# A hand-searched order for the first 930 operations, replaced by another

## The chip, the cores and the metric

The kernel runs on one core of a Trainium2 chip. The metric is the device time of one launch in microseconds (us), the median of three runs. The engines are TensorE (PE; PEld is its weight load), VectorE (DVE), ScalarE (ACT), GpSimd (POOL) and SyncE (SP), which issues all loads and stores here.

## What is computed

A linear attention with a decaying state, and two gated layers behind it, all in float32 accuracy:

```python
for t in range(S):                                    # B, H, S, D = 4, 8, 768, 48
    cur = einsum('bhd,bhe->bhde', u * k[t], v[t])
    y[t] = einsum('bhd,bhde->bhe', r[t], state + cur)
    state = w[t][..., None] * state + einsum('bhd,bhe->bhde', k[t], v[t])
x  = y, transposed to (3072 tokens, 384)
x1 = ((x @ w_a) * (x @ w_b)) @ w_out                  # d_ff 1536
out = (max(x1 @ w_in, 0) ** 2) @ w_out2               # d_ff 2048
```

## The kernel before

**Attention** is done for 24 pairs of chunks of 64 time steps. For each pair the kernel loads `ef` (the decays, L281), `rk` (r and k transposed, L285), `nat` (r and k as they are, L289) and v in two layouts (`vs`, L292 and 293; `v`, L298). DVE forms the running products of the decays (a scan, L307) and their reciprocals (four L312); k and r are scaled by them (L316 and L326, on DVE or GpSimd), and the diagonal terms come from two products on `nat` (L337), a sum (L341) and two L350. PE makes the scores (L361, L362), a transpose of k (L372), the state's increment (L384, L386) and the result (L405, L406); DVE merges scores and diagonal (L367) and updates the state (L393 to L397); ACT copies the result out of PSUM (`ys`, L230), and SP stores it to DRAM (L417).

**The layers** take the tokens in blocks: 384, 256, 384 and four of 512 in the first, six of 512 in the second. A block's x is loaded from DRAM (L692), and held as two rounded float32 parts whose sum is x: ACT makes the high part `xh` (L230), and an L631 subtracts it to leave `xl`. Each product is then three matmuls instead of one (L431 to L433). In a block of the first layer there are twelve steps f. A step makes two products ("ua" and "ub"); ACT evacuates the first (L438), DVE multiplies it with the second (L442), ACT and DVE or GpSimd split the result into `gh` (L230) and `gl` (L454), and nine matmuls add it to three accumulators (L461 to L463, the "down" matmuls). The accumulators are evacuated at the block's end (L230 or L234) and stored (L688).

**The weights** are float64 words. A unit of weights serves a step; three loads bring it (L219), and seven operations decode it: two copies on ACT, a mask (L248), a shift (L252), an addition (L257), a copy on ACT, and a subtraction (L266) that leaves the low part. L257 and L266 go to DVE or GpSimd. All of the first layer's twelve units are decoded during block 0.

**The order.** The program first lists 2574 operations (`plan.add`), each with the engines that can do it, and a list scheduler (`Plan.run`) puts them in an order with times of its own. The first 930 in that order are then replaced by a table, `LEAD`: numbers of operations, in the order in which they are written into the program, with a letter for the engine (V DVE, A ACT, P POOL; without one it is PE or a DMA, of which there is one choice). The engines run what is written for them strictly in this order, SP too, and each instruction waits for its operands and for its buffer. The 930 reach to the second step of block 3, some 270 us into the run.

```python
lead = [(int(x.rstrip("VAP")), LETTER.get(x[-1])) for x in LEAD.split()]
led = {i for i, _ in lead}
order = [(0.0, i, e or next(iter(ops[i][1]))) for i, e in lead] + [x for x in order if x[1] not in led]
```

Of the kernel before, what the change touches and what calls it, by code (L numbers as in the profile page):

```python
# [49 lines left out]

LETTER = {"V": "DVE", "A": "ACT", "P": "POOL"}
LEAD = """
    0 4 34 5V 2573 31 6V 8V 7V 35 1 16P 36V 62 2572 17V 47P 9V 11P 2 37V 32 10P 696 48P 14A 12A 39V 38V 18V 24 40V 66
# [4 lines left out]
    926A 91 730A 90A 746 106V 927V 722V 108P 118A 105A 928 133V 131V 142V 723P 729A 92 114 737 116V 96 724A 929A 137V
    731V 931 125 747 119V 139P 930P 932A 732V 115 738 933V 733V 756 934 120A 725V 748 734A 135V 936 126 757 122 766
    935A 132V 130V 735P 943 739A 937V 138A 121A 938A 945 741V 740A 134V 939V 749A 148 742V 758 776 149A 751V 940 767  # L60
    750A 944A 743V 941 946V 744A 752V 159 942 145 144 952 745V 953A 947A 759A 954 753P 760A 150V 777 768 961 955V
    761V 963 786 948V 962A 754A 762V 949 770A 970 971A 778 136A 950 755V 763P 787 127 158 806 796 964V 769A 147V 972
    956A 979 951 965A 973V 771V 764A 957V 772V 780A 958 788 981 797 123 980A 765V 146 966V 773V 779A 974A 774A 798
    982V 988 781V 975V 990 151A 775V 782V 959 967 989A 789A 152A 960 983A 790A 991V 155 976 968 969 977 157 807 791V
    783V 784A 997 984V 808 792V 153 985 998A 978 999 785V 171V 793V 799A 992A 1000V 794A 801V 986 1006 800A 154 993V
    1007A 1008 795V 112A 1048 189 802V 994 1001A 1009V 987 1015 803V 1002V 809A 1016A 1010A 186 1017 172V 995 804A
    1011P 1018V 1003 173V 996 811V 1004 1012 805V 1005 1013 810A 812V 1024 1019A 143A 813V 217 188 156 190 1026 1020V
    160V 1021 1014 814A 1025A 1049A 187 221 815V 1022 1023 1027V 1050P 1033 164V 163V 161V 1028A 1029P 1035 1034A
    191V 1030 1036V 1051 170P 1037A 195V 162V 1031 1052A 1053 1038P 166V 167A 1032 1060 165V 1054V 193V 202P 1039
    1061A 1042A 192V 1062 203P 179 1069 168V 180A 232P 1063V 176 1055A 1071 1070A 1064A 169A 175 204V 194V 1056P 222V  # L70
    181V 1072V 251 196P 1078 178V 174A 1079A 218 219 1065P 197P 1057 1040 210 225V 1041 177 1080 1073A 224V 200A 233P
    198A 211A 220 247 1044V 234V 226V 1043 201P 1066 1058 207 1081V 223V 199P 1074P 1046A 182A 212V 183A 1067 1087
    1088A 206 1059 1082V 262P 228P 205A 227P 209V 1089 1083P 1075 1096 240 1068 1090V 229V 184 279 275 249 1091A 241A
    1097A 263V 208 1098 1076 252V 213A 215 248 1045 1092V 1084 1105 280V 231P 230P 290P 255V 1099V 264V 307 185 237
    242V 1107 1106A 1077 236 1108V 260V 1114 1085 235A 239V 276 1116 1093 1100A 318P 1101P 258P 1115A 214A 1086 216
    238 253V 281V 254V 1117V 303 277 250 1094 291P 1123 256V 243A 259P 292V 245 1102 1124A 1109A 1125 335 257V 1095
    283V 1126V 1110P 1132 308V 319V 1103 268 1133A 244A 1118A 269A 1111 1104 1119V 288P 1112 1127A 282V 284V 1134 246
    1165 261P 1135V 312V 309V 278 1128P 1113 266 267V 1141 1136A 285P 1120 305 1142A 1143 346P 1144V 286P 296 270V
    1121 297A 1150 347P 1166A 1122 1152 310V 1151A 1167P 1153V 1145V 265A 294 289P 304 311V 320V 331 1129 298V 271A
    1168 1137P 287P 293A 1130 272A 1138 363 313V 1146V 336V 1169A 1170 1147 1139 1131 340V 1171V 316P 295V 374P 1148  # L80
    1140 1177 359 273 348V 324 337V 314P 332 333 1178A 1154A 391 325A 315P 1179 322 361 306 1047 1155P 1180V 339V
    338V 317P 364V 1186 402V 323V 1149 1187A 342P 1188 341V 1156 375P 1195 1189V 1172A 1181A 1159A 299A 300A 1173P
    344P 301 274 1157 1197 403P 345P 343P 1196A 326V 368V 376V 419 1158 352 1204 365V 1161V 1190V 353A 321A 387 360
    367V 334 366V 350 1174 1182P 1198V 302 1205A 430V 1191P 1206 327A 351V 329 1160 431P 1163A 1175 389 1213 1207V
    392V 370V 1176 1183 1199A 1215 369V 1214A 328A 354V 395V 1216V 380 1192 394V 372V 1222 404V 396V 349A 373V 388
    330 381A 1200V 393V 1162 1164 415 1184 378 355A 371V 382V 390 357 1223A 1224 1185 1208A 377A 356A 1193 1231 447
    362 417 443 1209V 1225V 399V 358 416 1201 397V 1233 1232A 398V 1194 408 1202 1240 409A 1217A 379V 400V 432V 1218V
    1203 1210 475 1282 406 1211 1226A 420V 458V 1227V 383A 459V 1234V 401V 445 418 1219 410V 1212 384A 1228 1220 1242
    1221 1235V 407V 385 1241A 405A 1229 1249 471 444 1230 386 1236V 1243V 460V 503 1251 1250A 1244A 1283A 423V 486V
    448V 1237 1258 1238 1259A 1245V 1252V 1253V 1260 422V 1254V 1284V 1239 487V 1261V 1267 1246 1268A 1269 452V 424V  # L90
    427V 449V 450V 1255 1285 1286A 1270V 428V 1247 1287 514V 421V 425V 1262V 1288V 426V 1256 1248 1263V 1271A 1294
    429V 1257 1295A 1289A 1272V 451V 1264 436 1290V 437A 1265 1273
"""


# [853 lines left out]
```

## Time and profile before

| | before |
|---|---|
| time, median of 3 runs | 986.78 us (986.64 to 988.69) |
| the profiled execution | 984.9 us, span 983.1 us |
| mean granted PE clock | 0.977 |
| busy: PE | 935.7 us (95%) |
| busy: DVE | 505.2 us (51%) |
| busy: ACT | 387.6 us (39%) |
| busy: POOL | 384.0 us (39%) |
| HBM read, written | 71.95 MB, 14.16 MB |

The span runs from the first to the last instruction of the program; the launch's own time is a little longer. Busy shares are means over the whole span, and the stages differ: attention's first pairs and the decoding of weights stand at the start, and the second half is matmuls of the second layer. So windows are read beside the shares.

### The profile page before, as it was taken

The page shows a single profiled execution, that of the slowest core. Times are in us where ns is not written, and L with a number is a line of the kernel's source. Part 1 is how long each engine was busy: PE and PEld are TensorE (multiplying, and loading weights), DVE is VectorE, ACT ScalarE, POOL GpSimd, SP SyncE. Part 2 cuts the span into 40 slices and gives each one's busy share as a digit, 9 for nine tenths or more (in the row PEclk, how much of TensorE's full clock was granted, in tenths as well). Part 3 has the DMA queues.
Part 4 walks back from the last instruction along what each step waited for, and adds up shares of the span by engine and source line. Part 5 has one row for each costly group of instructions (what it writes and reads, how often), then busy time and mean ns, then how long its engine had stood idle before and what let it go on. Part 6 is the DMA issues. An engine that isn't in the chain of part 4 may idle for free.

```text
span 983.1 us, 15022 instructions
## 1 busy us (share of the span) xinstructions
PE 935.7 (95%) x5982; PEld 799.3 (81%) x5982; DVE 505.2 (51%) x652; ACT 387.6 (39%) x600; POOL 384.0 (39%) x295
## 2 busy tenths in 40 slices
PE   2469999999999999999999999999999999999997
PEld 2459989999888888888888888888888888888885
DVE  7999999999755455532211789621121211211211
ACT  2677743343223332323322676433333333333332
POOL 5533177820165556543122444333333333333332
PEclk9569999999999999999999999999999999999999
DMA  8997336555022432220103562010000100100001
GB/s 224 258 288 225 112 89 178 145 162 157 25 82 81 139 108 69 85 65 29 48 33 113 193 212 95 0 65 1 33 33 1 53 11 1 65 1 1 33 0 36
DMA packets 58031, 87.17 MB, mean 89 GB/s; under 512 B 23904, under 2 KB 34912, under 8 KB 57952
## 3 DMA queue, kind: packets, MB, share of 16 engines
q1 hardware_dynamic: 57952, 86.12, 28.8%
q8 instruction: 49, 0.80, 0.3%
q14 instruction: 30, 0.25, 0.1%
HBM read 71.95 MB, written 14.16 MB: 88 GB/s over the span
## 4 chain that ended last, share of the span: by engine, by line
PE 84%; DVE 6%; DMA 6%; issue 1%; SPq 1%; ACT 0%; DVEq 0%; ACTq 0%
PE pa L431 15%; PE pa L432 15%; PE pa L433 15%; PE acc L461 11%; PE acc L462 11%; PE acc L463 11%; DMA raw<-in_w1pk_dram 2%; PE sc L361 2%; PE yp L405 2%; DMA rk<-in_tpk_dram 2%; DMA xd<-ys 1%; DVE ef L312 1%; DVE z L252 1%; PE ds L386 1%; DVE w L266 1%
## 5 line engine op out<-in xcount | busy, mean ns | idle before, releaser
L454 POOL TENSOR_TENSOR gl<-a,gh 128x512 fp32r<-128x512 f32 (+2 forms) x158 | 209.2, 1324 | 468.2 <-ACT gh L230 465.5
L431 PE MATMUL pa<-xh,w 128*128 128x512 f32 (+2 forms) x792 | 296.0, 374 | 1.4 <-ACT a L438 0.6
L432 PE MATMUL pa<-xl,w 128*128 128x512 f32 (+2 forms) x792 | 293.6, 371 | 0.6 <-DVE xl L631 0.6
L433 PE MATMUL pa<-xh,w 128*128 128x512 f32 (+2 forms) x792 | 293.6, 371 | 0.0
L438 ACT ACTIVATE a<-pa 128x512 f32<-128x512 f32 (+2 forms) x180 | 102.1, 567 | 289.5 <-PE pa L433 228.2
L461 PE MATMUL acc<-gh,w 128*128 128x512 f32 (+2 forms) x540 | 205.5, 381 | 0.0
L463 PE MATMUL acc<-gl,w 128*128 128x512 f32 (+2 forms) x540 | 202.5, 375 | 0.0
L462 PE MATMUL acc<-gh,w 128*128 128x512 f32 (+2 forms) x540 | 202.4, 375 | 0.0
L442 DVE TENSOR_TENSOR a<-a 128x512 f32<-128x512 f32 x96 | 68.3, 712 | 254.3 <-ACT a L438 254.3
L230 ACT ACTIVATE gh<-a 128x512 fp32r<-128x512 f32 (+2 forms) x174 | 105.2, 606 | 182.6 <-DVE a L442 125.4
L431 PEld LDWEIGHTS pa<-xh,w 128*128 128x128 f32 x792 | 149.5, 189 | 26.4 <-DVE a L442 1.6
L432 PEld LDWEIGHTS pa<-xl,w 128*128 128x128 f32 x792 | 149.5, 189 | 23.3 <-issue 0.9
L433 PEld LDWEIGHTS pa<-xh,w 128*128 128x128 f32 x792 | 149.4, 189 | 23.0
L461 PEld LDWEIGHTS acc<-gh,w 128*128 128x128 f32 x540 | 101.4, 188 | 17.8 <-DVE o L234 0.4
L463 PEld LDWEIGHTS acc<-gl,w 128*128 128x128 f32 x540 | 101.5, 188 | 17.0
L462 PEld LDWEIGHTS acc<-gh,w 128*128 128x128 f32 x540 | 101.5, 188 | 16.2
L442 DVE TENSOR_TENSOR a<-a,pa 128x512 f32<-128x512 f32 (+2 forms) x84 | 50.5, 602 | 109.2 <-PE pa L433 101.7
L312 DVE RECIPROCAL ef<-ef 112x128 f32<-112x128 f32 x96 | 84.4, 919 | 0.3
L367 DVE COPY_PREDICATED ar<-csb,sc 64x512 f32<-64x512 int32 x48 | 35.3, 735 | 32.7 <-PE sc L362 30.8
L307 DVE TENSOR_TENSOR_SCAN ef<-ef,floor 112x520 f32<-112x520 f32 x24 | 34.9, 1456 | 19.6 <-DMA ef<-in_tpk_dram 19.6
L405 PE MATMUL yp<-ar,vs 112*48 112x64 f32 x384 | 30.3, 237 | 12.3 <-ACT ar L230 8.2
L405 PEld LDWEIGHTS yp<-ar,vs 112*48 112x48 f32 x384 | 25.9, 135 | 19.0 <-ACT ar L230 8.7
(71 smaller groups left out, 893.8 us busy)
## 6 DMA issues: line engine op xcount, KB each, us to landing
raw<-in_w1pk_dram SPq DMA_DIRECT2D x36, 384.0 KB, 6.8
raw<-in_w2pk_dram SPq DMA_DIRECT2D x32, 384.0 KB, 4.1
rk<-in_tpk_dram SPq DMA_DIRECT2D x24, 448.0 KB, 4.7
nat<-in_natpk_dram SPq DMA_DIRECT2D x24, 384.0 KB, 3.3
ef<-in_tpk_dram SPq DMA_DIRECT2D x24, 227.5 KB, 3.6
vs<-in_vpk_dram SPq DMA_DIRECT2D x48, 96.0 KB, 3.0
v<-in_v2pk_dram SPq DMA_DIRECT2D x48, 96.0 KB, 3.4
xd<-ys SPq DMA_DIRECT2D x48, 96.0 KB, 2.4
```

Of the source, the lines that this page charges most:

```text
L230: nc.scalar.activation(out=out, in_=in_, func=ACTF.Copy, **({} if scale is None else {"scale": scale}))
L312: nc.vector.reciprocal(out=hv(inv(p), C)[:, h0:h0 + 2], in_=hv(ext(p), C + 1)[:, h0:h0 + 2, 1:])
L405: nc.tensor.matmul(out=P[OD, cs], lhsT=vs[0:112, 0, es], rhs=ar[0:112, 0, cs], start=True, stop=True)
L431: nc.tensor.matmul(out=out, lhsT=blk(wh, k), rhs=h, start=(k == 0), stop=False)
L432: nc.tensor.matmul(out=out, lhsT=blk(wh, k), rhs=l, start=False, stop=False)
L433: nc.tensor.matmul(out=out, lhsT=blk(wl, k), rhs=h, start=False, stop=(k == KD - 1))
L438: nc.scalar.activation(out=a[:, 0:n], in_=P[:, 0:n], func=func, scale=scale)
L442: eng(e).tensor_tensor(out=a[:, 0:n], in0=a[:, 0:n], in1=b[:, 0:n], op=ALU.mult)
L454: eng(e).tensor_tensor(out=gl[:, 0:n], in0=g[:, 0:n], in1=gh[:, 0:n], op=ALU.subtract)
L461: nc.tensor.matmul(out=acc[d][:, c0:c0 + m], lhsT=blk(wh, d), rhs=gh[:, 0:m], start=first, stop=False)
L462: nc.tensor.matmul(out=o, lhsT=blk(wl, d), rhs=gh[:, 0:n], start=False, stop=False)
L463: nc.tensor.matmul(out=o, lhsT=blk(wh, d), rhs=gl[:, 0:n], start=False, stop=last)
```

## The change

The table `LEAD` is another one. It holds the same 930 operations, so all that changes is the order in which they are written and, for 52 of them, the engine: 23 go from POOL to DVE, 24 from DVE to POOL, four from DVE to ACT and one from ACT to DVE. The three splits of x that were on POOL (one piece of block 0, and blocks 1 and 2) are on DVE. The operations behind the table follow in the order they had. The first lines of the diff:

```diff
 LEAD = """
-    0 4 34 5V 2573 31 6V 8V 7V 35 1 16P 36V 62 2572 17V 47P 9V 11P 2 37V 32 10P 696 48P 14A 12A 39V 38V 18V 24 40V 66
-    25A 21 33 697 13V 67V 15V 20 49V 41P 97 78P 26V 42P 3 55 79P 51 698 19A 56A 23V 70V 93 109P 46P 80V 22 45A 699A
...
+    0 4 2 5V 2573 31 8V 9V 1 7V 16P 35 36V 62 2572 6V 17P 696 37V 11P 40V 3 47P 18V 10V 66 48V 24 67V 697 25A 14A 12A
+    13P 49V 21 39V 46P 68V 32 20 33 26V 78P 97 15P 698 38V 19A 79P 23V 42P 93 706 41V 43A 80V 109P 45A 55 71V 63 22
...
```

What that does to the engines is seen in their instructions, as they stand in the built program (line, operation, what it writes and reads, size, and how many alike follow each other).

DVE at the start, from the second pair's scan (L307) to the second pair's sum (L341), before:

```order
L307 SCALAR_TENSOR_TENSOR ef<-ef,floor 112x520
L337 TENSOR_TENSOR nat<-nat,u_sb 128x384
L312 RECIPROCAL ef<-ef 112x128 x4
L341 TENSOR_REDUCE dg<-nat 128x8
L312 RECIPROCAL ef<-ef 112x128
L350 TENSOR_TENSOR ar_88<-csb,dg 64x512
L307 SCALAR_TENSOR_TENSOR ef<-ef,floor 112x520
L350 TENSOR_TENSOR ar_88<-csb,dg 64x512
L341 TENSOR_REDUCE dg<-nat 128x8
```

and now:

```order
L307 SCALAR_TENSOR_TENSOR ef<-ef,floor 112x520
L312 RECIPROCAL ef<-ef 112x128 x3
L341 TENSOR_REDUCE dg<-nat 128x8
L316 TENSOR_TENSOR rk<-rk,ef 112x512
L337 TENSOR_TENSOR nat<-nat,u_sb 128x384
L307 SCALAR_TENSOR_TENSOR ef<-ef,floor 112x520
L341 TENSOR_REDUCE dg<-nat 128x8
```

The two diagonals (L350) have gone to GpSimd, and the scaling of k for the first pair (L316) has come from there; one L337 is exchanged for that of the other pair.

DVE from the last pieces of x for block 0 (`xl`, L631) to the first multiply of two products (L442), before:

```order
L252 SCALAR_TENSOR_TENSOR z<-z,raw_393 128x1152
L631 TENSOR_TENSOR xl<-xl,xh 128x3x128
L257 ISA z<-raw_393,z 128x2304
L266 TENSOR_TENSOR w_509<-z,w_509 128x1152
L326 TENSOR_TENSOR rk<-rk,ef 112x512
L312 RECIPROCAL ef<-ef 112x128 x2
L442 TENSOR_TENSOR a<-a,pa 128x384
```

and now:

```order
L631 TENSOR_TENSOR xl<-xl,xh 128x3x128
L252 SCALAR_TENSOR_TENSOR z<-z,raw_395 128x1152
L631 TENSOR_TENSOR xl<-xl,xh 128x3x128
L257 ISA z<-raw_395,z 128x2304
L266 TENSOR_TENSOR w_518<-z,w_518 128x1152
L312 RECIPROCAL ef<-ef 112x128
L442 TENSOR_TENSOR a<-a,pa 128x384
```

The second piece's split stands on DVE too now, and an L326 and an L312 less stand between the last split and the multiply.

ACT where the result of pair 2, the last of block 0, is copied out (`ys`, two copies) and the first piece of x is rounded (`xh`); `z`, `raw` and `w` are the decoding. Before:

```order
L230 ACTIVATE z<-raw_276 128x1152
L230 ACTIVATE w_441<-z 128x1152
L230 ACTIVATE raw_276<-raw_276 128x1152
L230 ACTIVATE ys<-yp 48x512
L230 ACTIVATE xh<-xl 128x3x128
L230 ACTIVATE raw_393<-raw_393 128x1152
L230 ACTIVATE ys<-yp 48x512
```

and now:

```order
L230 ACTIVATE ys<-yp 48x512
L230 ACTIVATE z<-raw_262 128x1152
L230 ACTIVATE xh<-xl 128x3x128
L230 ACTIVATE raw_262<-raw_262 128x1152
L230 ACTIVATE w_471<-z 128x1152
L230 ACTIVATE ys<-yp 48x512
```

The first `ys` has moved ahead of three decode copies, and the second ahead of the next unit's `raw`.

## Rows read from the trace of the kernel before

**Rows 1.** The page's slices: busy tenths in 40 equal parts of the span.

```profile
PE   2469999999999999999999999999999999999997
DVE  7999999999755455532211789621121211211211
```

**Rows 2.** Windows: stretch, length, busy of each engine (instructions), PE clock, DMA share, GB/s.

```profile
core 0: us, PE busy (x) PEld busy (x) DVE busy (x) ACT busy (x) POOL busy (x), PEclk, DMA share, GB/s
0.00:62.00 62.00, 23.35 (x330) 19.83 (x332) 56.34 (x76) 29.75 (x40) 33.63 (x33) 0.71 0.88 237
62.00:125.00 63.00, 61.75 (x413) 59.78 (x410) 60.65 (x72) 46.11 (x60) 16.18 (x7) 0.96 0.66 204
125.00:250.00 125.00, 124.31 (x1339) 118.45 (x1338) 119.98 (x182) 47.57 (x95) 63.34 (x52) 1.00 0.50 141
250.00:500.00 250.00, 250.00 (x1809) 207.55 (x1809) 116.78 (x159) 78.15 (x132) 115.59 (x92) 1.00 0.24 72
...
50.00:66.00 16.00, 7.37 (x60) 6.00 (x60) 15.74 (x21) 10.03 (x14) 5.17 (x3) 0.50 0.87 260
```

**Rows 3.** Timeline of PE: start us, length us, instruction, idle before and releaser.

```profile
63.89 0.66 PE L432 MATMUL pa<-xl,w 128*128 128x384 f32 x1 [0.57 <-DVE xl L631]
...
119.92 0.33 PE L461 MATMUL acc<-gh,w 128*128 128x384 f32 x1
...
120.44 0.33 PE L431 MATMUL pa<-xh,w 128*128 128x384 f32 x1
...
129.86 0.38 PE L431 MATMUL pa<-xh,w 128*128 128x256 f32 x1 [0.56 <-DVE a L442]
...
132.60 0.61 PE L384 MATMUL ds<-v,kn 128*48 128x96 f32 x5
```

**Rows 4.** Timeline of DVE from the last split of block 0's x.

```profile
63.19 0.55 DVE L631 TENSOR_TENSOR xl<-xl,xh 128x384 fp32r<-128x384 f32 x1
...
68.87 0.56 DVE L442 TENSOR_TENSOR a<-a,pa 128x384 f32<-128x384 f32 x1 [0.32 <-PE pa L433]
...
87.73 0.55 DVE L442 TENSOR_TENSOR a<-a,pa 128x384 f32<-128x384 f32 x1 [1.48 <-ACT z L230]
...
119.12 1.33 DVE L266 TENSOR_TENSOR w<-z,w 128x1152 fp32r<-128x1152 f32 x1
```

**Rows 5.** Timeline of DVE before that.

```profile
9.99 0.54 DVE L337 TENSOR_TENSOR nat<-nat,u_sb 128x384 f32<-128x384 f32 x1
...
17.36 1.61 DVE L350 TENSOR_TENSOR ar<-csb,dg 64x512 f32<-64x512 f32 x1
...
51.85 0.68 DVE L350 TENSOR_TENSOR ar<-csb,dg 64x512 f32<-64x512 f32 x1
```

**Rows 6.** Groups by form, DVE, 0 to 125 us: xcount | busy us, mean ns.

```profile
L312 DVE RECIPROCAL ef<-ef 112x128 f32<-112x128 f32 x23 | 19.9, 914 | 0.1
...
L266 DVE TENSOR_TENSOR w<-z,w 128x1152 fp32r<-128x1152 f32 x10 | 13.5, 1350 | 0.0
L257 DVE CUSTOM_DVE_ANT_0 z<-raw,z 128x2304 uint16<-128x2304 uint16 x8 | 10.8, 1353 | 0.1
...
L350 DVE TENSOR_TENSOR ar<-csb,dg 64x512 f32<-64x512 f32 x5 | 5.0, 1004 | 0.0
L454 DVE TENSOR_TENSOR gl<-a,gh 128x384 fp32r<-128x384 f32 x9 | 5.0, 553 | 0.0
...
L316 DVE TENSOR_TENSOR rk<-rk,ef 112x512 f32<-112x512 f32 x2 | 1.4, 683 | 0.0
```

**Rows 7.** Timeline of ACT, 44 to 62 us.

```profile
53.46 0.59 ACT L230 ACTIVATE ys<-yp 48x512 f32<-48x512 f32 x1
...
61.26 0.52 ACT L230 ACTIVATE xh<-xl 128x384 fp32r<-128x384 f32 x1 [2.49 <-DMA xl<-xd]
```

**Rows 8.** Groups by form, POOL, 0 to 125 us.

```profile
L257 POOL TENSOR_TENSOR z<-z,raw 128x1152 int32<-128x1152 int32 x4 | 13.0, 3250 | 23.1 <-DVE z L252 10.1 <-ACT ys L230 9.9 <-issue 3.2
```

**Rows 9.** Timeline of POOL.

```profile
16.75 1.67 POOL L316 TENSOR_TENSOR rk<-rk,ef 112x512 f32<-112x512 f32 x1 [1.10 <-DMA rk<-in_tpk_dram]
```

**Rows 10.** DMA issues, 110 to 170 us: count, KB, median us to landing.

```profile
v<-in_v2pk_dram SPq DMA_DIRECT2D x8, 96.0 KB, 3.0
```

More of the change, by code (lines that the diff above doesn't have):

```diff
@@ L52 @@
 LEAD = """
-    0 4 34 5V 2573 31 6V 8V 7V 35 1 16P 36V 62 2572 17V 47P 9V 11P 2 37V 32 10P 696 48P 14A 12A 39V 38V 18V 24 40V 66
-    25A 21 33 697 13V 67V 15V 20 49V 41P 97 78P 26V 42P 3 55 79P 51 698 19A 56A 23V 70V 93 109P 46P 80V 22 45A 699A
-    110P 63 716 69V 71V 68V 52 44V 706 27A 700A 701V 98V 64 128 57V 75P 72P 43A 29 54V 50A 86 707 73P 28A 702V 94 53
-    87A 76A 140V 717 703P 111V 102V 101V 99V 704A 58A 59A 83 124 708 100V 77P 82 104P 88V 726 705P 107A 709A 85V 710A
-    65 718 30 711V 141V 712V 727 74A 60 736 81A 719A 103V 713V 84 925 95 714A 728 129V 721V 113 117 715V 720A 61 89A
@@ L58 @@
[L58 to L92, printed above, removed]
+    0 4 2 5V 2573 31 8V 9V 1 7V 16P 35 36V 62 2572 6V 17P 696 37V 11P 40V 3 47P 18V 10V 66 48V 24 67V 697 25A 14A 12A
@@ new lines @@
+    13P 49V 21 39V 46P 68V 32 20 33 26V 78P 97 15P 698 38V 19A 79P 23V 42P 93 706 41V 43A 80V 109P 45A 55 71V 63 22
+    44P 56A 69V 699A 716 98V 700A 52 77V 701V 707 70V 73P 34 51 57V 75P 128 72P 27A 76A 708 28A 54V 50A 110P 82 94
+    702V 140P 111V 709A 86 53 64 99V 703P 124 100V 87A 29 85V 717 65 711V 83 58A 710A 141V 129V 704A 726 712V 74A 60
+    59A 88V 104P 30 718 705P 736 101V 84 81A 132V 925 713P 727 131V 102V 61 89A 719A 142V 91 926A 103V 720A 95 106V
+    113 927V 728 714A 721V 108V 90A 928 722V 117 92 118A 746 715V 114 96 116V 137P 931 107A 723P 119V 737 929A 730A
@@ new lines @@
+    729A 747 105A 731V 724A 115 125 930V 732V 932A 738 933V 733V 934 748 725V 734A 766 936 935A 133V 135P 756 739A
+    943 937V 735V 938A 126 945 741V 944A 749A 939V 130V 139P 940 159 740A 946V 941 757 751V 952 120A 776 134V 750A
+    742V 942 767 138A 148 954 752V 149A 953A 758 136A 743V 145 947A 777 961 955V 753P 744A 150V 768 956A 121A 962A
+    786 144 745V 754A 963 948V 759A 755V 760A 970 761V 787 957V 949 762V 971A 778 770A 950 171V 958 951 964V 763P 796
+    147V 972 965A 769A 806 959 973V 127 771V 960 143A 764A 979 172V 788 772V 981 966V 797 974A 980A 765V 780A 967
@@ new lines @@
+    773V 779A 988 975P 982V 774A 146 173V 781V 989A 990 983A 775V 189 798 782V 976 997 151A 789A 991V 807 783V 790A
+    968 122 999 791V 998A 158 984V 784A 792V 969 985 992A 808 977 800A 785V 978 188 155 986 993V 799A 987 793V 994
+    112A 995 801V 1006 1000V 794A 156 802V 810A 1008 996 795V 123 1007A 153 1001A 803V 186 809A 1015 190 1002V 804A
+    1009V 811V 1003 1017 805V 1010A 152A 154 1016A 1004 1011V 1024 812V 1018V 1012 1048 813V 1019A 1026 1025A 217
+    1020V 814A 1013 160V 221 1005 1021 815V 1014 187 1049A 1022 191V 1033 1027V 1023 1050V 1028A 1035 1034A 1029V
@@ new lines @@
+    161V 170P 1030 164V 1051 202P 1036V 1031 162V 168P 1037A 1053 1052A 192V 1038P 1032 1054V 1060 163V 203P 194V
+    1039 1061A 165P 1062 1055A 204V 1042A 193V 166P 1043 1040 1063V 157 1069 195V 179 180A 169A 1064A 175 196V 222V
+    1070A 1071 1056V 197V 176 1072V 199P 198A 1078 219 181V 167A 1065P 1057 251 178V 1080 232P 210 200A 174A 201P
+    233P 1044V 1066 247 177 225V 211A 1079A 224V 1041 220 1087 1073A 262P 182A 1081V 234V 229P 218 206 1046A 1088A
+    226V 223V 1089 1074P 209V 279 184 263P 207 1090V 1075 227V 1096 252V 1058 1098 183A 1097A 212V 205A 231P 240 1067
@@ new lines @@
+    1059 228P 1099V 290P 1082V 1076 1105 256V 208 1083P 241A 275 254V 230P 1068 248 237 1091A 213A 1092P 264V 253V
+    1077 1106A 1084 291P 255V 277 307 236 242V 1107 249 257P 1093 185 1114 1108V 215 239V 261P 250 1085 1115A 1116
+    235A 214A 1086 1117V 1094 280V 1123 1100A 303 1101V 238 216 258P 282V 281V 1124A 276 1125 284V 283V 243A 260P
+    244A 1095 245 1102 259P 1109A 1132 1126V 268 308V 1103 269A 1134 246 1110V 292V 318P 266 1133A 1118A 1135V 312V
+    319P 1141 305 1119P 285P 1111 1142A 1165 1104 270V 267V 1112 1127A 1120 1128P 296 1143 286P 1045 311V 1113 265A
@@ new lines @@
+    1150 287P 1144V 320V 297A 1129 331 288P 309V 1166A 278 310V 1121 1152 289P 1136A 294 1151A 1167V 335 304 336V
+    1130 271A 1168 1153V 1137P 298V 313P 1122 1138 1169A 1170 1145A 316P 363 293A 346V 1131 273 1146V 1177 340V 314P
+    272A 332 1171V 315P 324 295V 1147 325A 1179 1154A 274 347P 1178A 337V 1047 322 306 1180V 1155P 374P 359 333 338V
+    339V 317P 348V 1186 299A 341P 326V 391 342P 1139 1187A 1188 300A 323V 375P 321A 352 344P 1140 1148 360 387 376V
+    353A 1172A 1195 364V 350 343V 361 1173V 345P 1189V 366V 402P 1149 327A 351V 1156 1197 1181A 371P 1196A 365V 1159A
@@ new lines @@
+    370P 1157 1160 368V 1198V 1204 334 1161V 1182P 419 1174 367V 1158 1175 369V 354V 1190A 301 1206 1205A 328A 1191V
+    349A 403V 1183 1213 1163A 404V 447 373V 380 1184 1207V 302 372V 1192 388 362 381A 392V 1176 1215 1199A 1214A 396V
+    1164 1193 378 458V 1216V 395V 329 389 1200V 390 382V 1222 415 1185 417 1223A 393V 1224 355A 1208A 1225V 398V 357
+    356A 379V 1201 1231 394V 1194 358 1202 377A 1217A 1209V 330 1233 401V 1232A 416 1210 1234V 1240 397V 1282 1218V
+    400V 408 1203 1242 430V 1226A 420V 1241A 443 459V 1219 409A 1227V 1211 421V 406 431V 432V 1243V 475 399V 1249
@@ L93 @@
+    383A 410V 385 384A 1212 1250A 1251 445 418 422V 405A 1228 407V 386 1235A 1220 471 1283A 1258 1252V 444 1236V 460V
+    1229 1259A 1237 448V 503 1260 1284V 1162 1221 1238 423V 1244A 1267 1261V 1245V 1230 452V 1269 1253A 1268A 1254V
+    451V 1246 1239 1285 428V 486V 1270V 426V 1247 1286A 1287 424V 1262V 425V 514V 1255 1263V 1248 450V 1256 1271A
+    1294 429V 1272V 487V 427V 1288V 1257 1264 1289A 449V 436 1295A 1290V 437V 1265 1273
 """
```

## The prediction

> **What bounds the kernel now.** I read the slices of the page first [rows 1]: TensorE (PE) is at nine tenths from the fourth slice to the last, so what it loses lies in the first 75 us. The windows put figures on that [rows 2]: PE is busy 23.35 of the first 62 us, then 61.75 of 63, 124.31 of 125 and 250.00 of 250. From about 62 us on the time is a fixed queue of matmuls, so the end moves by as much as the start of the first large product moves, plus or minus what PE then waits. The third reading is who is full before that: VectorE (DVE) is, with 56.34 of 62 and 60.65 of 63 us; ScalarE (29.75) and GpSimd (33.63) are not, and DMA has 0.88 of its engines' time in the first window [rows 2]. So the start is the length of DVE's list ahead of the last split of x (L631), if the loads keep up. In the trace PE stops on exactly that split: its second matmul waits for `xl` [rows 3], and the split is the row at 63.19 us [rows 4]. The second place where DVE is just in time is the end of block 0: the last decoded weights are written by the L266 row from 119.12 to 120.45 us [rows 4], and the product that reads them starts at 120.44 [rows 3].
>
> The profiled execution took 984.9 us, 1.88 less than the median of the three runs, 986.78. The sum below is made against 984.9, and its difference is put on the median.
>
> **DVE's list up to the last split.** 57 operations of the table stand there before and 56 now. Eight leave: two L337 at 0.54 [rows 5], four of the five L350, the L257 at 1.35 and one L312 at 0.91 [rows 6]. The five L350 hold 5.0 us together, and the one that stays took 0.68 [rows 5], so the four that leave took 4.3: they were stretched, one of them to 1.61. Together 7.7 us. Seven come: two L316 at 0.68, an L337 at 0.54, two L350 at 0.68 as the one that stays, an L631 at 0.55 and another L312 at 0.91 [rows 4 to 6], together 4.7. The list is 2.95 us shorter, and the last split would end at about 60.8 us instead of 63.74.
>
> The loads must keep up with that. In the trace the ScalarE copy ahead of the split waits 2.49 us for the last piece of x to land, at 61.24 us; the store that this load waits for comes behind the `ys` copy at 53.46 [rows 7]. In the new ScalarE order the first `ys` of the pair stands ahead of three decode copies that it followed, and the second has one fewer ahead of it (about 1.25 us). With what its producer gains on DVE I take the load as 2 to 3 us earlier, so about 58.7 us; the split needs it by 60. That is cover of about one microsecond, and the first rival is that it's not there. On GpSimd the L350 that arrive cost little, but it also gets the L257 of weights unit 1, at 3.25 us against 1.35 on DVE [rows 6, 8]. It lies beside DVE's work: the weights it serves are wanted only at the second step.
>
> **The first product.** In the trace 5.13 us pass from the end of the split (63.74) to the start of the first multiply L442 (68.87), in which PE makes two products, the first at the lower level: the granted clock is 0.50, 1.2 GHz, from 50 to 66 us [rows 2, 4]. DVE filled that time with other work and waited 0.32. In the new order only L257, L266 and one L312 lie between: 1.35 + 1.35 + 0.91 = 3.6. DVE then waits 5.13 - 3.6 = 1.5 us, **1.2 more than before**. What is queued behind that multiply is the whole decode of weights, so I count the loss in full.
>
> **The end of block 0.** Up to the last L266 DVE has 118 operations before and 117 now. Beyond those named, an L326 (as L316, 0.68) and an L454 (0.55) leave, an L266 (1.35, from GpSimd) and an L454 come, and the L312 of both lists cancel: 8.0 us out, 5.7 in, so 2.3 shorter. Against the 1.2 lost at the first product stands the wait of 1.48 at the multiply of 87.73 us [rows 4]: the same multiply now finds more DVE work ahead of it and PE some 2 us earlier, and I take 1.2 of it as gone. So the last weights are ready 2.3 us earlier. PE has three matmuls fewer behind it when it gets there, 0.52 us, the distance from 119.92 to 120.44 [rows 3]; this work is only moved back, so PE's lead is 1.8.
>
> **After block 0.** At 129.86 us PE was idle for 0.56 behind a DVE multiply [rows 3], with an L326 and an L316 ahead of it. Both have gone to GpSimd, and I count **0.5 us** won. PE lost 0.69 in the whole window of 125 to 250 and nothing in the next [rows 2], so no more can be won there. For the rest, the new order brings no product or down-matmul nearer to the DVE instruction that it waits for than the margin it has in the trace, so I count nothing. The three splits of x that were on GpSimd add about 2.7 us to DVE (0.55 for 128 columns [rows 4], five times that in all for the 256 and 384 of blocks 1 and 2); L316, L326, L337 and L350 of the later pairs go to GpSimd for it.
>
> Sum: 1.8 + 0.5 = **2.3 us** less: 982.6 for the profiled execution, 984.5 as a median.
>
> **The unknown price** is how a two-operand DVE instruction fares beside GpSimd, for the new table puts eight such on DVE before the end of block 0. The trace shows both ends: an L350 of 0.68, and one of 1.61 while GpSimd ran its L316 from 16.75 to 18.42 [rows 5, 9]. I take the short end, since the decode groups' means (L266 1.35, L454 0.55, L316 0.68) show no stretching although GpSimd is at work half of that time [rows 2, 6]. The long end is 0.93 each, 7.4 for all eight. The Trainium skill, GPSIMD Engine Reference, Key points, says that GpSimd shares its SBUF interfaces with VectorE and contends with DVE instructions that have two SBUF inputs. Taken for all eight, that rule would make it 992; the trace agrees for some instructions, not for most.
>
> **Rivals.**
> - Bigger gain. The wait at the first product costs nothing because PE, not DVE, then sets block 0: PE keeps the lead of the split. 2.95 + 0.5, and the last 0.3 of the wait at 87.73: 3.75, so 983.0, and down to 981.3 if DVE also loses 1.7 less of the 5.7 us in which it's idle in the first window [rows 2]. For it: PE waited nowhere for long in 62 to 125 [rows 2]. Against: the last L266 was just in time [rows 4].
> - Less. The last piece of x lands when it did, at 61.24 [rows 7]: copy 0.52, split 0.55, so the split ends at 62.4, 1.4 earlier, and 0.7 of it is left after block 0: **986.1**. For it: DMA is at 0.88 and in order of issue. Against: its store is issued earlier.
> - Slower, by contention. Four of the eight are stretched by 0.93, 3.7 us, which is 1.4 more than the gain: **988.2**. It decides from three (2.8 us). For it: five L350 at a mean of 1.00 [rows 6]. Against: the same L350 are what leaves.
> - Slower or the same, by the queue of SP. The load of `v` for pair 5 now stands behind the first store of block 0's result, which it did not. From the product at 129.86 to the first reader of that `v` at 132.60 are 2.74 us [rows 3]; the new PE order puts a product more and the pair's scores between. The load needs about 1.5 to be issued behind that store and 3.0 to land [rows 10]. So it's hidden by little; at 5 us to land PE would wait about 2, which leaves 986.5, and at 8 us it is slower.
> - The change doing nothing of what it says is excluded by the order itself: all 930 operations are there, and no split of x is left on GpSimd.
>
> **How the numbers follow.** About 2 us (0.2%) is what a measurement of this kernel can tell from no change, so faster means below 984.8, and my forecast lies 0.3 inside that. Forecast (1.3 to 3.3 us gained) 0.44, of which 0.27 counts as faster and 0.17 as the same; bigger gain 0.23; less 0.17; contention 0.11; the SP queue 0.05. Faster: 0.27 + 0.23 = 0.50. Same: 0.17 + 0.17 = 0.34. Slower: 0.11 + 0.05 = 0.16. The range runs from the low end of the bigger gain, 981.3, to just under the contention case, 988.0; the likeliest case alone is 983.5 to 985.5.
>
> **What would show it.** Right: the last L631 of the first three ends near 60.8 us; the first L442 waits about 1.5 us; the last L266 of block 0 ends near 118.2; the window of 125 to 250 shows PE at 124.8 or more; L316 and L350 on DVE have means near 0.7. Wrong: the copy ahead of the last split waits for its load until 61 us; L316 or L350 on DVE at 1.2 or more; PE idle over 1 us before an L384 near 131 us; or DVE waits that the trace of before doesn't have anywhere between 10 and 60 us.

## The result, and the profile after

The changed kernel is slower: 991.68 us (median of six runs, 990.83 to 991.73) against 986.06 for the kernel before on the same chip, a ratio of 1.0053, 95% interval 1.0041 to 1.0065. I had forecast 984.5, with a range to 988.0. Its profiled execution took 990.83 us, span 989.0; against the 983.1 before, that is 5.9 us more.

The windows of the changed kernel, same columns as [rows 2]:

```profile
0.00:62.00 62.00, 22.05 (x305) 18.83 (x305) 56.56 (x69) 27.66 (x38) 35.13 (x33) 0.80 0.78 227
62.00:125.00 63.00, 59.06 (x391) 54.32 (x392) 61.55 (x72) 46.17 (x60) 17.70 (x9) 0.92 0.64 203
125.00:250.00 125.00, 124.66 (x1346) 119.75 (x1346) 119.62 (x174) 49.10 (x101) 60.61 (x52) 1.00 0.52 146
250.00:500.00 250.00, 250.00 (x1817) 208.53 (x1816) 124.11 (x169) 77.48 (x132) 112.65 (x91) 1.00 0.25 72
...
50.00:66.00 16.00, 7.88 (x93) 6.14 (x89) 15.74 (x21) 10.99 (x14) 5.01 (x2) 0.50 0.75 206
```

From 125 us on nothing is lost: PE has 124.66 us, 0.35 more than before, and then 250.00 again. The loss lies in the first two windows. DVE is as busy as before there (56.56 us against 56.34), but with 69 instructions in the place of 76: they take longer on average. The timeline of DVE (start, length, instruction; idle before it and its releaser only where there was some) shows which:

```profile
28.10 1.61 DVE L350 TENSOR_TENSOR ar<-csb,dg 64x512 f32<-64x512 f32 x1
29.72 1.50 DVE L248 TENSOR_SCALAR raw<-raw 128x1152 int32<-128x1152 int32 x1
...
41.87 2.97 DVE L337 TENSOR_TENSOR nat<-nat,u_sb 128x384 f32<-128x384 f32 x1
...
66.23 0.55 DVE L631 TENSOR_TENSOR xl<-xl,xh 128x384 fp32r<-128x384 f32 x1
...
67.97 2.35 DVE L266 TENSOR_TENSOR w<-z,w 128x1152 fp32r<-128x1152 f32 x1
...
72.28 0.56 DVE L442 TENSOR_TENSOR a<-a,pa 128x384 f32<-128x384 f32 x1 [1.10 <-PE pa L433]
...
118.16 2.19 DVE L266 TENSOR_TENSOR w<-z,w 128x1152 fp32r<-128x1152 f32 x1
...
125.36 1.32 DVE L266 TENSOR_TENSOR w<-z,w 128x1152 fp32r<-128x1152 f32 x1
```

and the timeline of GpSimd (POOL) shows what ran beside them:

```profile
27.97 1.19 POOL L326 TENSOR_TENSOR rk<-rk,ef 112x512 f32<-112x512 f32 x1 [3.67 <-PE yp L406]
29.11 1.49 POOL L350 TENSOR_TENSOR ar<-csb,dg 64x512 f32<-64x512 f32 x1
...
41.46 2.96 POOL L266 TENSOR_TENSOR w<-z,w 128x1152 fp32r<-128x1152 f32 x1
...
66.74 2.35 POOL L326 TENSOR_TENSOR rk<-rk,ef 112x512 f32<-112x512 f32 x1 [4.22 <-DMA rk<-in_tpk_dram]
...
117.58 1.55 POOL L350 TENSOR_TENSOR ar<-csb,dg 64x512 f32<-64x512 f32 x1
```

Read the two fences in pairs. The L337 at 41.87 takes 2.97 us, where one takes 0.54 [rows 5]. GpSimd's L266 ends at 41.46 + 2.96 = 44.42, and the L337 ends at 44.84, 0.42 later: it did its work when GpSimd was through. So with the L350 at 28.10 (GpSimd to 29.16, DVE to 29.71), the mask L248 at 29.72 (30.60 and 31.22), the L266 at 67.97 (69.09 and 70.32) and at 118.16 (119.13 and 120.35). The pair in rows 5 and 9 reads the same way: GpSimd to 18.42, the L350 to 18.97. None of these waits is idle time: the profile shows them as longer instructions. The groups by form of DVE, 0 to 125 us, columns as [rows 6], carry them in their means:

```profile
L266 DVE TENSOR_TENSOR w<-z,w 128x1152 fp32r<-128x1152 f32 x10 | 16.2, 1619 | 0.0
...
L248 DVE TENSOR_SCALAR raw<-raw 128x1152 int32<-128x1152 int32 x12 | 10.4, 865 | 0.1
...
L350 DVE TENSOR_TENSOR ar<-csb,dg 64x512 f32<-64x512 f32 x3 | 3.8, 1276 | 0.0
L316 DVE TENSOR_TENSOR rk<-rk,ef 112x512 f32<-112x512 f32 x4 | 3.5, 868 | 0.0
...
L312 DVE RECIPROCAL ef<-ef 112x128 f32<-112x128 f32 x20 | 17.5, 918 | 0.1
```

Against the same groups before [rows 6], L266 went from 1350 to 1619 ns and L316 from 683 to 868; the reciprocal stayed (914, 918).

To count such waits I took for every DVE instruction the time from the later of its start and its predecessor's end to its own end, less the usual duration of its form; what is left over 0.12 us beside a GpSimd instruction is a wait. Up to the end of block 0's last L266, in us:

| | before | changed |
|---|---|---|
| the instructions at their usual durations | 108.9 | 108.3 |
| waits behind GpSimd (count) | 2.7 (4) | 10.9 (13) |
| idle, and other stretching | 8.8 | 7.4 |
| end of the last L266 | 120.45 | 126.69 |

The waits grew by 8.2 us, more than the 6.2 by which the end moved; the rest of the list and the idle time got shorter. Up to the last split the waits are 2.7 and 7.05, and it ends at 66.78 in the place of 63.74. PE follows it, columns as [rows 3]:

```profile
66.83 0.69 PE L432 MATMUL pa<-xl,w 128*128 128x384 f32 x1 [1.61 <-DVE xl L631]
...
126.90 0.33 PE L431 MATMUL pa<-xh,w 128*128 128x384 f32 x1
```

This is again the second matmul that waits for `xl` [rows 3], 2.94 us later; and the product for the last weights starts 0.22 us after the L266 at 125.36 has ended, where it started at 120.44 before.

### The profile page after: what moved, and what is told of

It is laid out like the page before. It is cut to its first block, busy times and chain, and to the rows that moved or that the text cites. A ratio compares the mean times of both kernels' runs of the same rounds, so it can differ in the third digit from the quotient of the medians.

```text
span 989.0 us, 15011 instructions
## 1 busy us (share of the span) xinstructions
PE 938.0 (95%) x5982; PEld 800.5 (81%) x5982; DVE 513.0 (52%) x648; ACT 388.2 (39%) x603; POOL 383.1 (39%) x296
## 4 chain that ended last, share of the span: by engine, by line
PE 87%; DVE 6%; DMA 4%; issue 2%; SPq 1%; POOL 0%; ACT 0%; DVEq 0%; ACTq 0%; POOLq 0%
PE pa L431 16%; PE pa L433 15%; PE pa L432 15%; PE acc L461 11%; PE acc L462 11%; PE acc L463 11%; PE sc L361 2%; PE yp L405 2%; DMA raw<-in_w1pk_dram 2%; DVE ef L312 1%; PE kt L372 1%; DMA csb<-in_cst_dram 1%; PE ds L386 1%; DVE z L252 1%; DMA vs<-in_vpk_dram 1%
## 5 line engine op out<-in xcount | busy, mean ns | idle before, releaser
L454 POOL TENSOR_TENSOR gl<-a,gh 128x512 fp32r<-128x512 f32 (+2 forms) x154 | 205.4, 1334 | 463.1 <-ACT gh L230 460.0
L442 DVE TENSOR_TENSOR a<-a 128x512 f32<-128x512 f32 x96 | 68.5, 713 | 253.9 <-ACT a L438 253.9
L230 ACT ACTIVATE gh<-a 128x512 fp32r<-128x512 f32 (+2 forms) x178 | 107.4, 603 | 200.4 <-DVE a L442 129.3
L442 DVE TENSOR_TENSOR a<-a,pa 128x512 f32<-128x512 f32 (+2 forms) x84 | 50.5, 602 | 105.1 <-PE pa L433 97.8
L312 DVE RECIPROCAL ef<-ef 112x128 f32<-112x128 f32 x96 | 84.7, 920 | 0.3
L350 POOL TENSOR_TENSOR ar<-csb,dg 64x512 f32<-64x512 f32 x39 | 47.6, 1219 | 11.2 <-DVE dg L341 9.3
L307 DVE TENSOR_TENSOR_SCAN ef<-ef,floor 112x520 f32<-112x520 f32 x24 | 36.2, 1509 | 21.6 <-DMA ef<-in_tpk_dram 19.0
L337 POOL TENSOR_TENSOR nat<-nat,u_sb 128x384 f32<-128x384 f32 x17 | 21.2, 1246 | 51.6 <-DVE nat L337 49.4
```

The source lines that it names most:

```text
L230: nc.scalar.activation(out=out, in_=in_, func=ACTF.Copy, **({} if scale is None else {"scale": scale}))
L312: nc.vector.reciprocal(out=hv(inv(p), C)[:, h0:h0 + 2], in_=hv(ext(p), C + 1)[:, h0:h0 + 2, 1:])
L350: eng(e).tensor_tensor(out=hv(AR[p % 2][rows, c, :], C), in0=ident[rows, rows].rearrange("p (o t) -> p o t", o=1).to_broadcast([C, H, C]), ...
L442: eng(e).tensor_tensor(out=a[:, 0:n], in0=a[:, 0:n], in1=b[:, 0:n], op=ALU.mult)
L454: eng(e).tensor_tensor(out=gl[:, 0:n], in0=g[:, 0:n], in1=gh[:, 0:n], op=ALU.subtract)
```

## The experiments

**The theory**, "exclusion": a DVE instruction with operands in SBUF and a GpSimd instruction don't run at the same time, and the later waits for the rest of the earlier one. So the loss is made by which instructions meet. **The rivals**: "engines" (the 52 operations with another engine make the lists worse), "splits" (the three splits of x on DVE are the load), and a longer list or a later load. Waits and ends below are counted as above. In the kernels made from a table one line longer, line numbers are higher by one. Where a diff shows entries of one engine only, these are that engine's entries in their order, without those of the others between them. All ratios are against runs of the kernel before beside it.

**One swap.** Two neighbours on GpSimd, the L266 of weights unit 0 that the L337 had waited for and the L257 of unit 1, change places in the changed table; the rest is word for word the same.

```diff
-104P 705P 713P 137P
+104P 713P 705P 137P
```

> One edit to the changed table: on GpSimd the L266 of weights unit 0 and the L257 of unit 1 trade places; DVE, PE, ScalarE and SP have the same instructions in the same order, no engine changes. Theory 'exclusion' (a DVE instruction with operands in SBUF and a GpSimd instruction don't run at the same time, the later one waits for the rest of the earlier): the L337 of 41.87 us, which took 2.97 us beside that L266, takes 0.5, the last split of x ends 2.4 us earlier, and the time falls by 2 to 3, to about 989. Rival 'list' (what each engine has in its list, and the order on PE and DVE, made the change slower): nothing of that is touched, 991.7 within 0.8. Rival 'splits' (the three L631 on DVE cost 2.7 us): also 991.7.

Measured: 989.15 us against 985.52, ratio 1.0031 (1.0019 to 1.0043). DVE's timeline has the L337 (here L338) at its own length again, and the last split 2.73 us earlier:

```profile
41.55 0.55 DVE L338 TENSOR_TENSOR nat<-nat,u_sb 128x384 f32<-128x384 f32 x1
...
63.50 0.55 DVE L632 TENSOR_TENSOR xl<-xl,xh 128x384 fp32r<-128x384 f32 x1
```

No instruction changed its engine, and DVE's order is the same: "engines" and "splits" can't make this step. The last L266 ends at 124.4, 2.3 us earlier.

**GpSimd's order, in 16 of its first 26 places, then in 60 of all 83.** Only the order of GpSimd's own instructions is another; the other four engines keep the changed table.

```diff
-16P 17P 11P 47P 13P 46P 78P 15P 79P 42P 109P 44P 73P 75P 72P 110P 140P 703P 104P 705P 713P 137P 723P 135P
+16P 17P 11P 47P 46P 15P 44P 13P 78P 79P 42P 109P 110P 72P 75P 73P 140P 703P 104P 713P 705P 723P 137P 135P
```

> The changed table with the first 26 GpSimd instructions in another order (the same ones; the diagonals L350 of pairs 0 and 1 earlier, the two of e1 exchanged, one L350 behind an L257); the other four engines keep their lists and order word for word. Exclusion: most of the 7.0 us that DVE waited in this way ahead of the last split go, the split ends near 61 us (66.78 in the changed kernel, 60.8 in the prediction), and the time is 984 to 988. Lists and splits: 991.7 within 0.8.

> The changed table with all of its 83 GpSimd instructions in another order (the first 26 much as in e2), the other four engines word for word as in the changed table. In e2 DVE still waited 2.9 us between the first product and the last L266 of block 0 (at an L454, an L266, an L248 and an L266), at the places where the changed kernel has them. Exclusion: these go too, the last L266 ends near 119 us, and some 2 us more are won behind block 0; 982 to 985.5, at or under the kernel before, with all engine changes and the order of four engines untouched. Lists and splits: 991.7 within 0.8.

Measured: 987.03 us, ratio 1.0014 (1.0002 to 1.0025), with 4.2 us of waits; and for the longer one, which goes on with other places behind these 26, 984.32 us against 985.84, ratio 0.9985 (0.9976 to 0.9994), with 2.1 us. The last L266 of block 0 of the longer one, from DVE's timeline (L267 here):

```profile
119.14 1.32 DVE L267 TENSOR_TENSOR w<-z,w 128x1152 fp32r<-128x1152 f32 x1
```

It ends at 120.46, where the changed kernel's ended at 126.69. The whole loss is gone, and a little more, with all 52 operations on their new engines and the splits on DVE. Nor did GpSimd's results merely come earlier to a DVE that stood waiting for them: DVE's idle time up to the last L266 is 9.2 us here and 6.9 in the changed kernel; only the waits within its instructions fell. This was the run that settled the cause. Not all of the expectation came: the last L266 was to end near 119, and the 2 us to be won behind block 0 were not.

**The three splits back on GpSimd**, in the changed table:

```diff
-930V ... 1050V ... 1167V
+930P ... 1050P ... 1167P
```

> The changed table with the three splits of x (L631) back on GpSimd, in the places where they stand. Splits: 2.7 us of DVE's list go, 989. Exclusion: DVE's list gets shorter but GpSimd runs 6 us more that shut DVE out, so little comes of it: 991 within 1.5.

Measured: 989.84 us, ratio 1.0036 (1.0025 to 1.0047). The expectations of the two theories lay too close for this time to choose. The trace says more: the list up to the last L266 is only 0.47 us shorter (one of the three splits is in block 0), the waits fall from 10.9 to 8.1, and 2.5 us are lost again behind block 0 (the column "rest" of the table below: 864.7 against 862.2). So in block 0 the split is no load to speak of, and what moving it changed there is again who meets whom. The 2.5 us were not followed to their end; 0.5 of them is PE waiting for a split that GpSimd makes.

**The forms by themselves.** Behind the kernel's work seven DVE forms run three times each, alone, then once more beside 24 integer additions on GpSimd. The run's time is no measure here.

```diff
 plan.run()
+forms()                     # DVE: 7 forms x3
+tensor_copy(...)
+24 x gpsimd.tensor_tensor(add, int32 128x1152)
+forms()
```

> The kernel before, with a measurement behind its last operation: seven forms of DVE instruction, three of each, first with GpSimd idle and then while GpSimd runs 24 additions of 128x1152 (2.7 us each) one behind the other. Exclusion: the forms with two operands in SBUF (L337's product, L252's shift, L307's scan) take up to 2.7 us longer the second time, and GpSimd's additions wait for DVE in turn; a reciprocal, a sum and a product with an operand in PSUM take the same both times; for the mask L248, with one operand in SBUF, the changed kernel's trace (1.51 against 0.75) says that it waits too. If it is a shared bandwidth and no exclusion, all forms of the first kind are longer by a like factor and no more than about two.

The timeline of DVE, four of the seven alone and then beside GpSimd; `prp` is in PSUM, and xN is N instructions, from the start of the first to the end of the last:

```profile
991.27 1.94 DVE L768 RECIPROCAL pr<-pr 112x128 f32<-112x128 f32 x2
...
995.01 1.73 DVE L772 TENSOR_TENSOR pr<-pr,prp 128x384 f32<-128x384 f32 x3
996.77 1.74 DVE L774 TENSOR_TENSOR pr<-pr 128x384 f32<-128x384 f32 x3
998.43 2.35 DVE L776 TENSOR_SCALAR pr<-pr 128x1152 int32<-128x1152 int32 x3
...
1008.83 2.92 DVE L768 RECIPROCAL pr<-pr 112x128 f32<-112x128 f32 x3
...
1013.55 1.73 DVE L772 TENSOR_TENSOR pr<-pr,prp 128x384 f32<-128x384 f32 x3
1015.31 7.85 DVE L774 TENSOR_TENSOR pr<-pr 128x384 f32<-128x384 f32 x3
1023.08 9.33 DVE L776 TENSOR_SCALAR pr<-pr 128x1152 int32<-128x1152 int32 x3
```

and GpSimd's row for the same stretch:

```profile
1008.99 71.58 POOL L787 TENSOR_TENSOR pr<-pr,pr 128x1152 int32<-128x1152 int32 x24 [37.32 <-DVE pr L785]
```

The 24 additions stretch over 71.58 us, 2.98 us each; the shortest takes 2.61 and the longest 3.60, so they wait in their turn. The reciprocal and the product with an operand in PSUM take the same alone and beside it; so does the sum (1.73 both times). Three products from SBUF go from 1.74 to 7.85, three masks from 2.35 to 9.33, three shifts from 4.14 to 11.01, three scans from 3.79 to 10.64: 2.0 to 2.3 us more for each instruction, which is most of an addition. By the expectation a shared bandwidth was to stretch all four by a like factor of two at the most; the factors are 4.5, 4.0, 2.7 and 2.8. The theory as put above, "operands in SBUF", is too wide, since the reciprocal and the sum have theirs there as well. A price per instruction of DVE, like my 0.93, is thus the wrong form: the wait is what is left of the other's instruction.

The Trainium skill, "SBUF — State Buffer", section "SBUF: two separate sides", has the rule: the port pair that the two engines share is an exclusive lock, held for the whole instruction by whichever starts first, among GpSimd's instructions and those of DVE that have two SBUF inputs or run in a mode that uses both ports. The trace agrees, with 2.97 us for the L337 and the rows above; in which mode the mask with its one SBUF operand ran, no run here shows.

**The engines of before in the changed order.** The 52 letters are put back, and nothing else.

> The new order of the changed table, but each operation on the engine that it had before (all 52 changes of engine undone). Rival 'engines' (the 52 changes put the wrong work on DVE): about 986. Exclusion: the order was made with the changed engines, and with the old ones more of DVE's instructions stand beside a GpSimd instruction, and the list is no shorter; slower than the changed kernel, 994 to 1000. Rival 'lists' with both order and engines mattering a little: 988 to 992.

Measured: 993.04 us, ratio 1.0075 (1.0060 to 1.0090). "Engines" had it at the time of before, and falls. But the time lies just below the range of "exclusion" (994 to 1000) and just above that of "lists" (988 to 992), and the reason given fails for block 0: up to the last L266 this kernel is 4.2 us earlier than the changed one (122.5), with 5.6 us of waits in the place of 10.9. It loses 5.6 us more behind block 0, where PE is busy for 370.64 of the 375 us from 125 to 500 (374.66 in the changed kernel) and waits most for DVE's multiplies (2.4 us, four times). That these multiplies were late because of GpSimd is not shown. So the run speaks against "engines", and not for "exclusion".

**GpSimd's order in the table of before**, 65 of 82 places, so that nothing meets up to the last L266; the first twelve:

```diff
-16P 47P 11P 10P 48P 41P 78P 42P 79P 109P 46P 110P
+16P 47P 48P 11P 10P 46P 42P 78P 79P 41P 109P 110P
```

> The table of before with its GpSimd instructions in another order, the other engines word for word as before. Exclusion: the kernel before has 2.7 us of such waits up to the last L266 of block 0 (four of them), and more behind it where DVE is just in time; 981 to 984. If the exclusion only matters where the change brought it, 985.5 within 0.8.

A miss. Measured: 985.60 us, ratio 0.9999 (0.9988 to 1.0009). The waits did go, all of them, and the last split ends at 62.25, 1.5 us earlier. But the clock stepped up at 68.0 us, 0.5 later than before, and DVE was 1.9 us more idle: 0.9 of it at an instruction of the state update at 29.84 us (L393) that waits for PE, and 0.9 at the first multiply (0.32 in [rows 4]; L443 is L442):

```profile
68.28 0.56 DVE L443 TENSOR_TENSOR a<-a,pa 128x384 f32<-128x384 f32 x1 [1.22 <-PE pa L434]
```

So the last L266 ends only 0.57 us earlier, and that was lost again behind block 0. The 2.7 us of waits in the kernel before cost it nothing that could be had by taking them alone away.

**Meetings made on purpose, in the table of before.** Each moves one DVE instruction by two places, so that a split of x comes due while GpSimd has the L257 of the unit that DVE has just shifted. In the first the shift (L252) goes up, ahead of an L350 and the split:

```diff
-721V 715V 106V 927V 722V 133V
+721V 715V 722V 106V 927V 133V
```

> The table of before with one edit: on DVE the L252 of weights unit 2 (52.92 us) moves up two places, ahead of the L350 of 51.85 and the L631 of 52.45. No list changes, no engine changes, no wait of one operation for another is added. In the kernel before, the GpSimd L257 that this L252 releases (54.48 to 57.16) lies beside two reciprocals, a sum and the two merges L367. Exclusion: it now runs from about 53.8, a DVE instruction with operands in SBUF (the L631) is in its way and waits for all of it; the last split ends 2.5 to 3.5 us later (66 to 67), and the time is 988 to 989.5. Rival 'lists': the same instructions on the same engines with the same total, 985.7 within 0.8.

A miss: 986.11 us against 986.06, ratio 1.0001 (0.9989 to 1.0012). No DVE instruction waited; GpSimd did. DVE's timeline, and under it GpSimd's:

```profile
52.04 0.68 DVE L351 TENSOR_TENSOR ar<-csb,dg 64x512 f32<-64x512 f32 x1
52.64 0.54 DVE L632 TENSOR_TENSOR xl<-xl,xh 128x384 fp32r<-128x384 f32 x1
```

```profile
52.34 3.40 POOL L258 TENSOR_TENSOR z<-z,raw 128x1152 int32<-128x1152 int32 x1 [8.78 <-ACT raw L231]
```

GpSimd came due at 52.34, in the middle of DVE's L350, and DVE's next instruction still went ahead of it; GpSimd's ended 0.72 later than the 2.68 that it needs. The second moves the split down, so that a reciprocal, which the probe showed to run beside GpSimd, stands ahead of it:

```diff
-721V 715V 106V 927V 722V 133V
+721V 715V 106V 722V 133V 927V 131V
```

> The table of before with one edit the other way: on DVE the first L631 (52.45 us in the kernel before) moves down two places, behind the L252 of unit 2 and the reciprocal L312 that follows it. In e9 no collision came, since DVE had its L350 and L631 back to back when the GpSimd L257 became ready, and it was GpSimd that waited (3.40 us instead of 2.68). Exclusion, sharpened so (the one that asks first goes, and DVE asks for its next instruction while one still runs): now the L257 becomes ready while DVE is in the L252, starts during the reciprocal, which needs nothing of it, and the L631 behind it waits for the rest, 1.5 to 2.5 us; the last split ends at 64.5 to 66.5 (63.74 and 62.42 in the kernels without that wait). Of that the time shows less, by what PE's step to the higher clock gives back: 986.5 to 989. Rival 'lists': no wait on the L631, split near 62.4 to 63.7, 986.0 within 0.8.

Measured: 988.55 us against 985.63, ratio 1.0027 (1.0016 to 1.0039). DVE's timeline, then GpSimd's:

```profile
53.99 0.94 DVE L313 RECIPROCAL ef<-ef 112x128 f32<-112x128 f32 x1
54.86 2.85 DVE L632 TENSOR_TENSOR xl<-xl,xh 128x384 fp32r<-128x384 f32 x1
```

```profile
54.29 3.01 POOL L258 TENSOR_TENSOR z<-z,raw 128x1152 int32<-128x1152 int32 x1 [9.38 <-ACT raw L231]
```

The reciprocal runs beside GpSimd at its usual 0.9; the split waits until 57.30 and takes 2.85 in the place of 0.54. The waits double (5.4 us), the last split ends at 66.72 and the last L266 at 124.0, 3.0 and 3.5 later. Half of the loss of the change (2.9 of 5.6 us) is made here in the kernel before, with one DVE instruction two places further down and not one engine changed.

**A third table**, of the same 930 operations, laid out by durations from the traces and with the exclusion as a rule (47 engines differ from before). Its first line:

```diff
-    0 4 34 5V 2573 31 6V 8V 7V 35 1 16P 36V 62 2572 17V 47P 9V 11P 2 37V 32 10P 696 48P 14A 12A 39V 38V 18V 24 40V 66
+    0 31 2573 4 5V 62 35 1 32 2572 2 16P 47P 48P 17P 11P 36V 6V 9V 37V 67V 40V 38V 7V 8V 39V 10V 18V 696 697 66 24
```

> A table of the same 930 operations ordered anew, with 47 other engines than before (37 from DVE to GpSimd, ten the other way), set so that DVE and GpSimd seldom want SBUF at the same time: DVE's list is shorter by what moves, and the waits stay few. Exclusion, reckoned with the unstretched durations of the two traces and one engine waiting for the other: the last split ends near 57 us (63.74 before, 66.78 in the changed kernel), the last L266 of block 0 near 114 (120.45 before); 975 to 981, under both kernels. If DVE's list and its waits are not what sets the first 125 us, 985 or more.

Measured: 981.46 us against 985.84, ratio 0.9960 (0.9947 to 0.9974). It beats both kernels, but is 0.5 above the range that I expected, and its ends came 3 to 4 us later than reckoned (60.26 for 57, 117.96 for 114). Its windows, columns as [rows 2]:

```profile
0.00:62.00 62.00, 27.37 (x342) 23.29 (x343) 54.08 (x74) 30.56 (x42) 35.22 (x35) 0.85 0.90 258
62.00:125.00 63.00, 61.77 (x418) 59.92 (x417) 61.94 (x75) 46.15 (x61) 19.55 (x11) 0.98 0.59 183
```

DVE does 74 instructions in 54.08 us (69 in 56.56 in the changed kernel) with 0.8 us of waits, and PE is busy for 4.0 us more of the first 62 us than before. Since DVE's list is shorter here too, this run shows what the rule is good for, and doesn't tell the theories apart.

All kernels made from a table, in us; the first column as a ratio to before. "Clock" is the time from which the granted PE clock is 1.00, worked out from windows of one microsecond; "rest" is the time from the start of the product that reads block 0's last weights (120.44 before [rows 3], 126.90 in the changed kernel) to the end of the span:

| kernel | ratio | waits to last L266 (count) | last split ends | clock | last L266 ends | rest |
|---|---|---|---|---|---|---|
| before | 1 | 2.7 (4) | 63.74 | 67.5 | 120.45 | 862.7 |
| changed | 1.0053 | 10.9 (13) | 66.78 | 71.5 | 126.69 | 862.2 |
| one swap | 1.0031 | 7.2 (11) | 64.05 | 69.7 | 124.4 | 863.0 |
| GpSimd order, 26 | 1.0014 | 4.2 (7) | 61.78 | 66.3 | 121.65 | 862.1 |
| GpSimd order, 60 | 0.9985 | 2.1 (4) | 62.12 | 68.1 | 120.46 | 862.2 |
| splits on GpSimd | 1.0036 | 8.1 (9) | 65.8 | 71.5 | 124.2 | 864.7 |
| engines of before | 1.0075 | 5.6 (6) | 65.15 | 70.9 | 122.5 | 867.7 |
| before, GpSimd order | 0.9999 | 0 | 62.25 | 68.0 | 119.88 | 863.5 |
| before, first meeting | 1.0001 | 1.6 (2) | 62.42 | 68.7 | 120.28 | 863.0 |
| before, second meeting | 1.0027 | 5.4 (5) | 66.72 | 71.8 | 124.0 | 862.3 |
| third table | 0.9960 | 0.8 (3) | 60.26 | 64.2 | 117.96 | 861.7 |

The waits alone don't give the time. In the table of before, 0, 1.6 and 2.7 us of them make no difference that the runs can tell, and 5.4 us make 0.27%; with the engines of before in the changed order, 5.6 us go with the longest time of all, most of which is lost behind block 0.

## Why the prediction was wrong

The two places that bound the kernel were read rightly: PE stops on the last split in both kernels and starts the product of the last weights within 0.3 us of them, and with the second of these places (6.2 us later) the end moved (5.9 us).

**The step that failed is "the list is 2.95 us shorter", with the choice of the short end for the unknown price.** Both have one root.

- The four L350 that leave were taken at 4.3 us. That is the time they took, but of the 5.0 us of the five, 1.85 were waits behind GpSimd. A wait belongs to the meeting and doesn't leave with the instruction. Those that came were taken at their unstretched lengths. At usual durations on both sides the list to the last split is 54.93 before and 53.68 now: 1.25 shorter, not 2.95.
- The waits up to there then went from 2.7 to 7.05 us, which the sum had at no change. With the list 1.25 shorter and the waits 4.35 longer the split had to end 3.1 later; it ended 3.04 later, where the sum had it 2.95 earlier. The reason given was that the groups' means "show no stretching although GpSimd is at work half of that time". It was 0.4 of it (49.8 of 125 us [rows 2]), and the means showed that the old order seldom let the two meet; not that meeting is cheap.
- The long end, 0.93, was no bound either. It was what was left of GpSimd's instruction in one meeting [rows 5, 9]; the L337 shows 2.42.
- The price was called unknown, but the kernel has the rule in its source. `Plan.run` starts no DVE operation that is marked `port=True` while GpSimd is at work, and no GpSimd operation while such a one runs (`ported`, `PORT`). Marked are the forms that the probe found waiting (the scan, the products of L337, the mask and the shift), and L316, L326, L350, L257, L266, L454 and the splits; the reciprocals, the sum, the merge and the state update are not. The table `LEAD` replaces the order that was made by this rule, so it binds nothing there. The third table was laid out by such a rule, and has 0.8 us of waits.
- The rival "slower, by contention" had the mechanism, but looked for it on the eight instructions that are new on DVE. Only three of the thirteen waits fall on such (1.84 us); the other ten, 9.1 us, fall on instructions that stood on DVE before too and now meet others. Its 988.2, and the 992 for all eight that lies close to the result, came from the wrong instructions: that 992 was near is luck.

The other terms:

- The load of the last piece of x didn't come 2 to 3 us earlier (58.7 forecast). It was issued at 57.58 (56.76 before) and landed at 62.13, 0.9 later than before, but DVE was later still, and the copy behind it waited for nothing. The row of ScalarE's timeline, as [rows 7]:

```profile
63.63 0.51 ACT L230 ACTIVATE xh<-xl 128x384 fp32r<-128x384 f32 x1
```

- The wait at the first multiply was 1.10, forecast 1.5.
- The last L266 ended at 126.69, forecast 118.2.
- After block 0, 0.5 us was to be won, and 0.5 was (862.7 to 862.2 in the table, one trace each). The SP queue, the fifth case, cost nothing that can be seen.
- "The end moves by as much as the start of the first large product" held for this change, but it isn't a rule: two of the runs on the table of before had the last split 1.3 and 1.5 us earlier and ended where they had.

Of the signs named ahead, "L316 or L350 on DVE at 1.2 or more" was the one that came true (L350 at 1276 ns). "DVE waits that the trace of before doesn't have" did come, but not as idle time, where I would have looked for them.

## What to carry to other kernels

Price an instruction of DVE or GpSimd at its shortest row, and count the rest of longer rows as waits of a meeting: they leave only if the meeting does. When an order is changed, lay the two engines' SBUF instructions side by side over the new times before anything else, since a short DVE instruction behind a 3 us one on GpSimd costs what is left of that; reordering GpSimd alone was worth 0.68% in the changed kernel, and nothing in the kernel before. Read the scheduler's own rules before you let a table override them. And don't look for these waits in idle time: see whether busy time per instruction has grown.
